# Two mixture layers behind a linear attention: the stretch around the second routing, reordered

## The chip, the core and the metric

One core of one Trainium2 chip runs the whole program. The metric is device microseconds of one execution; three runs of the kernel before are shown. The engines are PE (TensorE: matrix products, and transposes as products with an identity), DVE (VectorE), ACT (ScalarE), POOL (GpSimd) and SP (SyncE, which here issues DMAs). Each takes its own instructions in order, and waits on semaphores that the others and the DMAs raise.

## The reference, cut to what matters

The input goes through three layers. The first is a linear attention (8 x 8 heads, 576 positions, 64 wide) with a norm of each row. The second is a mixture of 8 experts in which each of 4608 tokens takes the expert with the highest score. The third is a mixture with a capacity:

```python
    cap = N // E
    logits = x @ w_gate
    order = np.argsort(-logits.flatten())
    ...
        if assigned[tok] >= 0 or counts[e] >= cap:
            continue
        assigned[tok] = e
    ...
        h = np.maximum(x[mask] @ w1[e], 0.0)
        out[mask] = h @ w2[e]
```

The third layer's assignment needs the logits of all tokens, so it needs the result of the second layer for all of them. "The second routing" is this assignment.

## The kernel before, in words

**Products.** Every fp32 product is made of three: hi x hi, lo x hi and hi x lo, of operands that are split into a rounded half (`whi`, `xh`, `hh`) and a rest (`wlo`, `xl`, `hl`). ACT makes the first halves, DVE the rests. A layer of an expert is `layer1_g` (lines 669 to 671, then relu) and `layer2_g` (lines 711 to 713, then a copy out of PSUM at line 717). An expert of the second layer has 608 slots, worked on in two chunks: chunk 0 has 256 columns (2 tiles of 128 rows), chunk 1 has 352 (3 tiles, the last of 96 rows). After a chunk's second layer, `rows_y` transposes the result back to rows (line 729), scales it (line 731), adds the token's number (line 732) and writes each tile to the buffer `ybuf` in HBM (line 734). The third layer gathers its rows from `ybuf` by a table of slots, `tab2`.

**The second routing.** It runs on DVE, with small products on PE between: `da_start` finds each expert's range of logits and spreads it to all partitions with a product (line 1060, operand `dg`); eight calls of `da_round` narrow a threshold per expert (2 of them, WARM, while the last expert's logits are not in yet, and 6, ROUNDS); `da_choice` takes the choice; `table2` makes the table, with three products for running counts (lines 1131 to 1133) and two halves of 20 products each (line 1167). The last instruction that makes the table is line 1182.

**What PE does meanwhile.** The second layers of the last two experts (e6 and e7, numbers 6 and 7) are kept back for this, in the generator `second()`; the last expert's first layers are in `first7()`. `stream` hands them out in pieces: a call `pe(us)` records products for about that many microseconds into PE's order, at that place. The tables TFILL, WFILL and PW say how much at which place. So the order of all engines is fixed when the program is built, by these numbers; the kernel uses no scheduler (`manual_schedule`). The splits of the last expert's hidden values (`hl`, line 1473) are DVE work that is put into the list LATER, and POPS says how many are taken out in each round, between the round's comparisons and its counts.

**The branch.** If the first assignment fails, a slow general way follows, in an `If` (line 1556) that is not entered with these inputs. All five engines load the flag, compare and branch past the body. `expect("gen")` marks a branch hint, which the program carries as an instruction at its start on the engines listed.

**After the branch.** POOL gathers the first expert's rows (five indirect DMAs, line 618), DVE makes three weight rests that were held back (line 550, list CAST), which frees the buffers for SP's next weight loads (line 528), PE runs `warm(NWARM)`: that many transposes of the identity (line 843) whose result nobody reads. Then the gathered tiles are transposed (line 636) and the third layer's first products follow.

Of the kernel before, what the change touches and what calls it, by code (L numbers as in the profile page):

```python
# [27 lines left out]

TFILL = (5.5, 0.35, 0.35, 2.0, 6.4, 100.0)

POPS = (1, 1, 2, 2, 2, 2)

WFILL = (4.2, 0.35, 0.35)

PW = (0, 0.8, 2.9, 2.1)

NWARM = 45

ASIDE = (1, 5, 5, 5, 3)

# [35 lines left out]
def fused_kernel(ctx, tc, q, k, v, g_norm, emb, tau, w1, w2, wgate, v1, v2, out):  # L76
# [28 lines left out]
    def mk(pool, shape, dtype, name, **kw):  # L105
        if pool is mp:
            pool = MP[name in MP0]
        return pool.tile(shape, dtype, name=name, **kw)
# [423 lines left out]
    def wcast(n=1, eng=None, ahead=3, later=None):  # L532
        for _ in range(n):
            if WS["cast"] >= len(WQ):
                return
            wload(WS["cast"] + 1)
            key = WQ[WS["cast"]][0]
            raw = RAW.pop(key)

            i = WS["cast"] // (RING // 2)  # L540
            wp = WP[(i + (i > 2 * E - 2)) % 2]
            hi = mk(wp, [128, 1024], F32R, "whi")
            lo = mk(wp, [128, 1024], F32R, "wlo")
            nc.scalar.copy(hi, raw)  # L544
            WT[key] = (hi, lo)
            WS["cast"] += 1
            up = WS["cast"] + ahead

            def rest(eng, lo=lo, raw=raw, hi=hi, up=up):
                eng.tensor_tensor(lo, raw, hi.bitcast(F32), op=OP.subtract)  # L550
                wload(up)
            if later is None:
                rest(eng or V)
            else:
                later.append(rest)
# [143 lines left out]
    def layer2_g(e, c, dp, mid=None):  # L699

        N = WID[0][c]
        if dp == 0:
            YT[e, c] = mk(mp, [128, KD, COLS[c]], F32, f"yT{c}")
        hh, hl = HT[0, e, c]
        ps = mk(psum, [128, 2, 512], F32, "mm")
        for t in range(2):
            o = ps[:, t, :N]
            d = (2 * dp + t) * 128
            for kf in range(KF):
                a, b = (w[:, d:d + 128] for w in wb(0, e, kf))  # L710
                nc.tensor.matmul(o, a, hh[:, kf, :N], start=(kf == 0), stop=False)  # L711
                nc.tensor.matmul(o, a, hl[:, kf, :N], start=False, stop=False)  # L712
                nc.tensor.matmul(o, b, hh[:, kf, :N], start=False, stop=(kf == KF - 1))  # L713
                yield 3 * N / 2400
            if mid and t == 0:
                mid()
        nc.scalar.copy(YT[e, c][:, 2 * dp:2 * dp + 2, :N], ps[:, :, :N])
# [4 lines left out]
    def rows_y(e, c, eng=V):  # L722

        y = YT[e, c]
        for (t, n) in tiles_of(c):
            o = 128 * t - 256 * c
            pt = mk(psum, [128, KD, 128], F32, "tp")
            for kd in range(KD):
                nc.tensor.transpose(pt[:n, kd, :], y[:, kd, o:o + n], ident)
            yr = mk(mp, [128, YP], F32, "yr", bufs=4)  # L730
            nc.scalar.activation(yr[:n, :HD], pt[:n].rearrange("p a b -> p (a b)"), AF.Copy, scale=gts[:n, e * SC + t:e * SC + t + 1])
            eng.tensor_copy(yr[:n, HD:].bitcast(I32), tabi[:n, e * SC + t:e * SC + t + 1].to_broadcast([n, YP - HD]))
            r0 = e * SL + 128 * t
            nc.sync.dma_start(ybuf[r0:r0 + n, :], yr[:n])
            yield 0.43
# [69 lines left out]
    def logits_w(e, c):  # L805
        N = WID[0][c]
        i = e - (E - ND)
        parts = [H7[0][:, :, 256 * c:256 * c + N]] if e == E - 1 else [h.bitcast(F32)[:, :, :N] for h in HT[0, e, c]]
        pl = mk(psum, [128, 512], F32, "sm")
        for kf in range(KF):  # L810
            g = kf % 4
            for x, p in enumerate(parts):
                nc.tensor.matmul(pl[32 * g:32 * g + 32, :N], W2G[0][:, i, kf - g:kf - g + 4, :].rearrange("p k e -> p (k e)"),
                                 p[:, kf, :], start=(kf < 4 and x == 0), stop=(kf >= 4 and x == len(parts) - 1),
                                 tile_position=(0, 32 * g))
        lgT = mk(mp, [128, C1 - 256], F32, "lgT")
        nc.scalar.copy(lgT[:, :N], pl[:, :N])
        return lambda: rows_l(e, c, lgT, 40)
# [5 lines left out]
    def stream(g):  # L824

        owed = [0.0]

        def pe(us):
            owed[0] += us
            while owed[0] > 0:  # L830
                d = next(g, None)
                if d is None:
                    owed[0] = 0.0
                    return
                owed[0] -= d
        return pe
# [113 lines left out]
    pe = stream(f0)  # L950
# [86 lines left out]
    def da_start(n, pe):  # L1037

        lm = mk(mp, [128, NCOL, E], F32, "rA")
        V.scalar_tensor_tensor(lm[:, :n], vneg[:, :n, None].to_broadcast([128, n, E]), -2.0, L[:, :n], op0=OP.mult, op1=OP.add)  # L1040
        mm = mk(mp, [128, 2, E], F32, "mmx")
        V.tensor_reduce(mm[:, 0], lm[:, :n].rearrange("p c e -> p e c"), axis=AX.X, op=OP.min)
        V.tensor_reduce(mm[:, 1], L[:, :n].rearrange("p c e -> p e c"), axis=AX.X, op=OP.max)
        pe(PW[3])
        pm = mk(psum, [128, 512], F32, "sm")
        for i in range(2):
            nc.tensor.transpose(pm[:E, 128 * i:128 * i + 128], mm[:, i], ident)
        V.tensor_reduce(st[:, 0:1], pm[:E, 0:128], axis=AX.X, op=OP.min)
        V.tensor_reduce(st[:, 3:4], pm[:E, 128:256], axis=AX.X, op=OP.max)
        V.tensor_tensor(st[:, 4:5], st[:, 3:4], st[:, 0:1], op=OP.subtract)  # L1050
        V.scalar_tensor_tensor(st[:, 0:1], st[:, 4:5], -0.25, st[:, 0:1], op0=OP.mult, op1=OP.add)
        V.tensor_scalar(st[:, 4:5], st[:, 4:5], 1.25, 1e-12, op0=OP.mult, op1=OP.max)
        V.reciprocal(st[:, 1:2], st[:, 4:5])
        V.tensor_scalar(st[:, 2:3], st[:, 4:5], 1.0 / J, None, op0=OP.mult)
        dg = mk(mp, [E, 3, E], F32, "dg")
        V.tensor_tensor(dg, ident[:E, None, :E].to_broadcast([E, 3, E]), st[:, 0:3, None].to_broadcast([E, 3, E]), op=OP.mult)
        ones8 = mk(mp, [128, NCOL, E], F32, "rB").rearrange("p a e -> p (a e)")[:E, :128]
        V.memset(ones8, 1.0)
        pb = mk(psum, [128, 512], F32, "sm")
        nc.tensor.matmul(pb[:, :3 * E], ones8, dg.rearrange("p a b -> p (a b)"), start=True, stop=True)  # L1060
        V.tensor_copy(lw.rearrange("p a b -> p (a b)"), pb[:, :3 * E])
# [324 lines left out]
    e6, e7 = E - 2, E - 1  # L1386
# [27 lines left out]
    def under(pe, t, asides, n=1):  # L1414
        def fill(i):
            for _ in range(0 if i else min(n, len(asides))):
                asides.pop(0)(V)
            pe(t[i])
        return fill
# [32 lines left out]
    pe = stream(f7)  # L1452
    pe(PW[2])
    da_start((E - 1) * SC, pe)
# [3 lines left out]

    def second():
        prev = None  # L1460
        for e, c in ((e6, 1), (e6, 0), (e7, 1), (e7, 0)):
            yield from layer2_g(e, c, 0)
            if prev is not None:
                yield from rows_y(*prev)
            yield from layer2_g(e, c, 1)
            prev = (e, c)
            if e == e6:
                N = WID[0][c]
                HT[0, e7, c] = [mk(mp, [128, KF, COLS[c]], F32R, f"h{p}{c}") for p in "hl"]
                for f in range(4):  # L1470
                    h, hh, hl = (x[:, 2 * f:2 * f + 2, o:o + N] for x, o in zip([H7[0], *HT[0, e7, c]], (256 * c, 0, 0)))
                    nc.scalar.copy(hh, h)
                    LATER.append(lambda eng, h=h, hh=hh, hl=hl: eng.tensor_tensor(hl, h, hh.bitcast(F32), op=OP.subtract))  # L1473
            if (e, c) == (e6, 0):
                wcast(3, later=CAST)
                while len(LATER) > 4:
                    LATER.pop(0)(V)
            if (e, c) == (e7, 1):
                while LATER:
                    LATER.pop(0)(V)  # L1480
        yield from rows_y(*prev)

    def expect(label):

        tc.mark_branch_hint_location(label, 0, engines=[mybir.EngineType.PE, mybir.EngineType.SP])

    s2_ = second()
    pe = stream(s2_)
    pe(PW[0])
    a = logits_w(e7, 1)  # L1490
    pe(PW[1])
    a()
    for r in range(ROUNDS):
        da_round(under(pe, TFILL, LATER, POPS[r]))
    da_choice()
# [118 lines left out]
    while CAST:  # L1614
        CAST.pop(0)(V)
    warm(NWARM)
    xtiles(1, 0, 0, 2)
# [50 lines left out]
```

## Time and profile before

| | us |
|---|---|
| median of 3 runs | 1119.45 |
| the three runs | 1116.06, 1119.45, 1123.03 |
| the profiled execution | 1119.71 |
| its span, first to last instruction | 1117.6 |
| around the span | 2.1 |

PE is busy for 95% of the span, DVE for 55%, ACT for 41%, POOL for 25%. The mean granted clock of PE is 0.976 of full speed; it shows 1.0 in most of the span, and 0.5 in a few short stretches. The stretch that the change touches lies between 550 and 690 us: the second routing runs from 551 to 666, the branch follows, and the third layer's first product starts at 681.3.

### The profile page before, as it was taken

The page shows a single profiled execution, that of the slowest core. Times are in us where ns is not written, and L with a number is a line of the kernel's source. Part 1 is how long each engine was busy: PE and PEld are TensorE (multiplying, and loading weights), DVE is VectorE, ACT ScalarE, POOL GpSimd, SP SyncE. Part 2 cuts the span into 40 slices and gives each one's busy share as a digit, 9 for nine tenths or more (in the row PEclk, how much of TensorE's full clock was granted, in tenths as well). Part 3 has the DMA queues.
Part 4 walks back from the last instruction along what each step waited for, and adds up shares of the span by engine and source line. Part 5 has one row for each costly group of instructions (what it writes and reads, how often), then busy time and mean ns, then how long its engine had stood idle before and what let it go on. Part 6 is the DMA issues. An engine that isn't in the chain of part 4 may idle for free. (4 is left out here: it accounts for less than half of the span.)

```text
span 1117.6 us, 20567 instructions
## 1 busy us (share of the span) xinstructions
PE 1061.9 (95%) x8380; PEld 982.8 (88%) x8380; DVE 617.1 (55%) x1275; ACT 453.7 (41%) x803; POOL 278.2 (25%) x363
## 2 busy tenths in 40 slices
PE   6988699999999999999999878999999999999998
PEld 6887698899999999999889768998989898989896
DVE  4467956777778786857557544433334242515140
ACT  2567536544445353545432222333324242414231
POOL 2011446516061423415001004030303030312101
PEclk9998799999999999999999998999999999999999
DMA  9999654443424243434111116334334342425201
GB/s 288 373 355 296 214 174 156 141 139 111 152 96 165 85 154 118 131 114 132 63 39 48 37 48 200 123 114 132 124 113 130 107 158 79 161 85 171 76 25 42
DMA packets 94517, 152.86 MB, mean 137 GB/s; under 512 B 11080, under 2 KB 52040, under 8 KB 94416
## 3 DMA queue, kind: packets, MB, share of 16 engines
q1 hardware_dynamic: 85456, 122.18, 33.0%
q0 software_dynamic: 8960, 29.30, 7.9%
q8 instruction: 67, 1.10, 0.4%
q14 instruction: 34, 0.28, 0.1%
HBM read 121.63 MB, written 29.82 MB: 136 GB/s over the span
## 5 line engine op out<-in xcount | busy, mean ns | idle before, releaser
L669 PE MATMUL mm<-xh,whi 128*128 128x256 f32 (+2 forms) x1024 | 312.6, 305 | 4.1 <-DVE hl L687 2.6
L670 PE MATMUL mm<-xl,whi 128*128 128x256 f32 (+2 forms) x1024 | 308.9, 302 | 1.0 <-DVE ti L646 0.7
L671 PE MATMUL mm<-xh,wlo 128*128 128x256 f32 (+2 forms) x1024 | 308.6, 301 | 0.0
L669 PEld LDWEIGHTS mm<-xh,whi 128*128 128x128 f32 x1024 | 196.0, 191 | 7.2 <-DVE hl L687 3.5
L670 PEld LDWEIGHTS mm<-xl,whi 128*128 128x128 f32 x1024 | 196.1, 191 | 1.7 <-DVE ti L646 1.1
L671 PEld LDWEIGHTS mm<-xh,wlo 128*128 128x128 f32 x1024 | 196.0, 191 | 0.0
L550 DVE TENSOR_TENSOR wlo<-wraw,whi 128x1024 fp32r<-128x1024 f32 x128 | 158.3, 1238 | 43.9 <-ACT whi L544 37.6
L711 PE MATMUL mm<-hh,whi 128*128 128x352 f32 (+1 forms) x512 | 160.0, 313 | 1.0 <-DVE rA L1138 1.0
L712 PE MATMUL mm<-hl,whi 128*128 128x352 f32 (+1 forms) x512 | 156.1, 305 | 3.8 <-DVE hl L1473 3.5
L713 PE MATMUL mm<-hh,wlo 128*128 128x352 f32 (+1 forms) x512 | 156.0, 305 | 0.0
L640 DVE TENSOR_TENSOR xl<-tp,xh 128x512 fp32r<-128x512 f32 (+2 forms) x80 | 51.5, 649 | 187.5 <-ACT xh L639 187.5
L544 ACT CAST whi<-wraw 128x1024 fp32r<-128x1024 f32 x128 | 133.4, 1044 | 0.0
L1606 POOL DMA_INDIRECT out<-yr,ti x40 | 39.3, 983 | 313.4 <-ACT yr L1604 291.1
L801 DVE SCALAR_TENSOR_TENSOR rc<-xg,big 128x512 bf16<-128x512 f32 x128 | 111.1, 868 | 2.6
L686 ACT ACTIVATE hh<-mm 128x512 fp32r<-128x512 f32 (+1 forms) x88 | 57.2, 650 | 113.0 <-PE mm L671 113.0
L712 PEld LDWEIGHTS mm<-hl,whi 128*128 128x128 f32 x512 | 98.5, 192 | 4.4 <-DVE hl L1473 3.8
L1593 PE MATMUL mm<-whi,hh 128*128 128x512 f32 x256 | 101.0, 394 | 0.0
L711 PEld LDWEIGHTS mm<-hh,whi 128*128 128x128 f32 x512 | 98.2, 192 | 2.9 <-DVE rA L1138 1.3
L1595 PE MATMUL mm<-whi,hl 128*128 128x512 f32 x256 | 100.4, 392 | 0.0
L1594 PE MATMUL mm<-wlo,hh 128*128 128x512 f32 x256 | 100.3, 392 | 0.0
L713 PEld LDWEIGHTS mm<-hh,wlo 128*128 128x128 f32 x512 | 98.3, 192 | 0.0
L687 DVE SCALAR_TENSOR_TENSOR hl<-mm,hh 128x512 fp32r<-128x512 f32 (+1 forms) x88 | 66.0, 750 | 48.5 <-ACT hh L686 48.3
(282 smaller groups left out, 1461.2 us busy)
## 6 DMA issues: line engine op xcount, KB each, us to landing
wraw<-in_moe_w SPq DMA_DIRECT2D x128, 512.0 KB, 3.8
kmain<-in_k SPq DMA_DIRECT2D x16, 576.0 KB, 10.7
vmain<-in_v SPq DMA_DIRECT2D x16, 576.0 KB, 11.1
xbuf<-xo SPq DMA_DIRECT2D x16, 528.0 KB, 7.4
ybuf<-yr SPq DMA_DIRECT2D x32, 260.0 KB, 2.5
qmain<-in_q SPq DMA_DIRECT2D x16, 512.0 KB, 10.9
xg<-in_moe_w SPq DMA_DIRECT2D x16, 256.0 KB, 3.9
xg<-in_moe_w_gate SPq DMA_DIRECT2D x8, 256.0 KB, 3.8
```

The costliest lines, as they stand in the source:

```text
L544: nc.scalar.copy(hi, raw)
L550: eng.tensor_tensor(lo, raw, hi.bitcast(F32), op=OP.subtract)
L669: nc.tensor.matmul(o, a, xh[:, kd, :N], start=(kd == 0), stop=False)
L670: nc.tensor.matmul(o, a, xl[:, kd, :N], start=False, stop=False)
L671: nc.tensor.matmul(o, b, xh[:, kd, :N], start=False, stop=(kd == KD - 1))
L711: nc.tensor.matmul(o, a, hh[:, kf, :N], start=(kf == 0), stop=False)
L712: nc.tensor.matmul(o, a, hl[:, kf, :N], start=False, stop=False)
L713: nc.tensor.matmul(o, b, hh[:, kf, :N], start=False, stop=(kf == KF - 1))
L801: V.scalar_tensor_tensor(junk, raws[i], 1.0, wgB[:, x], op0=OP.mult, op1=OP.mult, accum_out=w2g[:, i // KF, i % KF, x:x + 1])
L1593: nc.tensor.matmul(ps[:n, i, :], hh, a, start=(kf == 0), stop=False)
L1594: nc.tensor.matmul(ps[:n, i, :], hh, b, start=False, stop=False)
L1595: nc.tensor.matmul(ps[:n, i, :], hl, a, start=False, stop=(kf == KF - 1))
```

## The change

It has five parts. (1) `da_start` records about 2.0 us of products (PW[4]) between the range and the broadcast product. (2) `second()` takes the kept-back chunks in the order 0, 1, 0, 1 instead of 1, 0, 1, 0; the two places that depend on it follow. (3) POPS has 1 instead of 2 for the fifth round. (4) The hint is marked on ACT, DVE and POOL too, not only on PE and SP. (5) NWARM is 28, not 45.

```diff
-POPS = (1, 1, 2, 2, 2, 2)
+POPS = (1, 1, 2, 2, 1, 2)
-PW = (0, 0.8, 2.9, 2.1)
+PW = (0, 0.8, 2.9, 2.1, 2.0)
-NWARM = 45
+NWARM = 28
@@ da_start
         V.tensor_scalar(st[:, 2:3], st[:, 4:5], 1.0 / J, None, op0=OP.mult)
+        pe(PW[4])
         dg = mk(mp, [E, 3, E], F32, "dg")
@@ second
-        for e, c in ((e6, 1), (e6, 0), (e7, 1), (e7, 0)):
+        for e, c in ((e6, 0), (e6, 1), (e7, 0), (e7, 1)):
...
-            if (e, c) == (e6, 0):
+            if (e, c) == (e6, 1):
                 wcast(3, later=CAST)
                 while len(LATER) > 4:
                     LATER.pop(0)(V)
-            if (e, c) == (e7, 1):
+            if (e, c) == (e7, 0):
                 while LATER:
                     LATER.pop(0)(V)
@@ expect
-        tc.mark_branch_hint_location(label, 0, engines=[mybir.EngineType.PE, mybir.EngineType.SP])
+        tc.mark_branch_hint_location(label, 0, engines=[mybir.EngineType[n] for n in ("PE", "SP", "Activation", "DVE", "Pool")])
```

From line 1055 on, a line of the changed kernel has a number that is one higher.

The first place is PE's order in `da_start`, at the broadcast product (a piece of the difference; the rows between its two parts are the same in both).

```order
 L671 MATMUL mm<-xh_6483,wlo 128x256
 L1047 MATMUL sm<-ident,mmx 8x128 x2
-L1060 MATMUL sm<-dg,rB 128x24
 L669 MATMUL mm<-xh_6483,whi 128x256
 L670 MATMUL mm<-xl_6484,whi 128x256
@@ -2948,4 +2947,5 @@
 L670 MATMUL mm<-xl_6484,whi 128x256
 L671 MATMUL mm<-xh_6483,wlo 128x256
+L1061 MATMUL sm<-dg,rB 128x24
 L669 MATMUL mm<-xh_6483,whi 128x256
```

The broadcast product moved behind 15 products of 256 columns and four transposes of 96 rows, all of which stood behind it before.

The second place is DVE's order in a round in which PE waits for the split hidden values. Before, in the fourth round (`hl_7251` is chunk 1 of the last expert):

```order
L1084 SCALAR_TENSOR_TENSOR rB<-rB,rP 128x320
L1087 TENSOR_REDUCE ru<-rB 128x40
L1090 TENSOR_TENSOR rc<-ru,gridf 128x32x20 x2
L1473 TENSOR_TENSOR hl_7251<-big,hh_7250 128x704 x2
L1098 COPY rB<-sm 32x128
L1103 TENSOR_SCALAR jk<-sm 32x8
```

With the change, in the sixth and last round (`hl_7434` is the same chunk):

```order
L1085 SCALAR_TENSOR_TENSOR rB<-rB,rP 128x320
L1088 TENSOR_REDUCE ru<-rB 128x40
L1091 TENSOR_TENSOR rc<-ru,gridf 128x32x20 x2
L1474 TENSOR_TENSOR hl_7434<-big,hh_7433 128x704 x3
L1099 COPY rB<-sm 32x128
L1104 TENSOR_SCALAR jk<-sm 32x8
```

Three of that chunk's four pieces are now made here; PE's first product with `hl_7434` stands shortly before this round's counts, where before its first product with `hl_7251` stood right behind the third round's.

The third place is SP's order ahead of the branch. Before:

```order
L528 DMA wraw<-in_moe_w 128x4x256 x3
L734 DMA ybuf<-yr 128x520 x2
L734 DMA ybuf<-yr 96x520
L734 DMA ybuf<-yr 128x520 x4
L734 DMA ybuf<-yr 96x520
L734 DMA ybuf<-yr 128x520 x2
L1556 TENSOR_LOAD fli
```

With the change:

```order
L528 DMA wraw<-in_moe_w 128x4x256 x3
L734 DMA ybuf<-yr 128x520 x4
L734 DMA ybuf<-yr 96x520
L734 DMA ybuf<-yr 128x520 x4
L734 DMA ybuf<-yr 96x520
L1557 TENSOR_LOAD fli
```

The last chunk written before the branch is now the one with three tiles, the last of 96 rows.

## Rows read from the trace of the kernel before

**Rows 1.** The page: the span, and PE's busy time.

```profile
span 1117.6 us, 20567 instructions
...
PE 1061.9 (95%) x8380; PEld 982.8 (88%) x8380; DVE 617.1 (55%) x1275; ACT 453.7 (41%) x803; POOL 278.2 (25%) x363
```

**Rows 2.** Timeline at the broadcast: start, duration, instruction, [idle before <- releaser].

```profile
554.87 0.17 DVE L1058 MEMSET rB<- 8x128 f32 x1
...
555.18 0.37 PE L1060 MATMUL sm<-dg,rB 8*128 8x24 f32 x2 [1.78 <-DVE rB L1058]
```

**Rows 3.** Timeline in the fourth round: the hidden values' rest, and PE.

```profile
624.11 1.69 DVE L1473 TENSOR_TENSOR hl<-big,hh 128x704 fp32r<-128x704 f32 x2
...
625.05 0.66 PE L712 MATMUL mm<-hl,whi 128*128 128x352 f32 x1 [3.46 <-DVE hl L1473]
```

**Rows 4.** Timeline of PE at the table's first products.

```profile
644.78 0.72 PE L1131 MATMUL mm<-Pf,ones 128*128 128x320 bf16 x1 [0.65 <-DVE Pf L1071]
...
647.94 0.39 PE L711 MATMUL mm<-hh,whi 128*128 128x256 f32 x1 [0.96 <-DVE rA L1138]
```

**Rows 5.** Windows: stretch; length, busy by engine, then PEclk, DMA share, GB/s.

```profile
556.00:561.00 5.00, 5.00 (x31) 4.99 (x30) 4.42 (x9) 1.72 (x5) 1.26 (x2) 0.66 0.01 2
624.00:629.00 5.00, 3.95 (x16) 3.95 (x17) 1.80 (x3) 0.71 (x1) 0.00 (x0) 0.66 0.00 0
648.00:653.00 5.00, 5.00 (x29) 5.00 (x30) 4.79 (x12) 1.59 (x2) 0.00 (x0) 0.66 0.00 0
...
682.00:687.00 5.00, 4.96 (x29) 4.96 (x30) 1.27 (x2) 0.61 (x2) 1.05 (x2) 0.66 0.28 107
...
670.00:675.00 5.00, 4.96 (x24) 4.99 (x25) 3.50 (x3) 0.00 (x0) 3.53 (x3) 0.50 0.53 157
676.00:677.80 1.80, 1.80 (x19) 1.80 (x18) 0.00 (x0) 0.00 (x0) 1.50 (x2) 1.00 0.98 327
```

**Rows 6.** Timeline around the last chunk ahead of the branch, on ACT, PE and SP.

```profile
658.00 0.68 ACT L731 ACTIVATE yr<-tp,gts 96x512 f32<-96x512 f32 x1
...
656.84 0.62 PE L729 MATMUL tp<-ident,yT 128*96 128x128 f32 x4
...
665.64 0.32 SPq L734 DMA_DIRECT2D ybuf<-yr  x1
```

**Rows 7.** Line 1556, the branch, by sequencer: durations ns min/median/max, first and last start.

```profile
L1556 SPq EVENT_SEMAPHORE  x9: 17/17/17, 667.5 to 669.9; - x9
...
L1556 PEldq EVENT_SEMAPHORE  x2: 51/51/51, 665.7 to 665.8; - x2
...
L1556 DVEq EVENT_SEMAPHORE  x2: 21/21/21, 669.9 to 670.0; - x2
...
L1556 PEldq COMPARE_BRANCH  x1: 397/397/397, 665.2 to 665.2; - x1
...
L1556 DVEq COMPARE_BRANCH  x1: 72/72/72, 666.7 to 666.7; - x1
...
L1556 SPq COMPARE_BRANCH  x1: 70/70/70, 667.0 to 667.0; - x1
```

**Rows 8.** Waits of SP's queue, 655 to 690: us in total, times, longest.

```profile
SPq L1556 <- SPq L1556: 2.3, 2, 1.9
```

**Rows 9.** Timelines of DVE, PE, POOL and SP from the table's end on.

```profile
665.79 0.20 DVE L1182 SCALAR_TENSOR_TENSOR tab<-si 128x40 int32<-128x40 f32 x1
...
670.04 7.98 PE L843 MATMUL sm<-ident 128*128 128x128 f32 x45 [4.62 <-DVEq L1556]
...
679.99 0.66 PE L636 MATMUL tp<-ident,xg 128*128 128x128 f32 x4 [1.53 <-DMA xg<-ybuf,tab]
681.32 0.39 PE L669 MATMUL mm<-xh,whi 128*128 128x256 f32 x1 [0.68 <-ACT xh L639]
...
670.86 1.34 POOL L618 DMA_INDIRECT xg<-ybuf,tab  x1 [34.87 <-SPq L1556]
...
671.34 0.40 SPq L528 DMA_DIRECT2D wraw<-in_moe_w  x1
```

**Rows 10.** The chain that ended last, at the gather: start, us, what.

```profile
672.51 7.43 DMA xg<-ybuf,tab
```

## The prediction

> **What bounds the kernel now.** I read the page first: PE is busy for 1061.9 of the span's 1117.6 us [rows 1], so the kernel can only get shorter by what PE loses, which is idle time and time at the lower of its two clock levels (granted 0.5, 1.2 GHz, against 1.0, 2.4 GHz). Then I went through the timeline of PE between 551 and 690 us for its idle times, and through the windows of the same stretch for the granted clock. There are three holes: 1.78 us before the broadcast product [rows 2], 3.46 us before the first product with the split hidden values [rows 3], and 0.65 and 0.96 us at the table's first products [rows 4]. After each hole the clock falls: the five microseconds around each show a granted clock of 0.66, with PE busy for all of them or for all but the hole [rows 5]. A window of 5 us at 0.66 does 3.3 us of work at full clock, so 1.7 us are lost beside the hole itself. The fourth place is the branch: PE has nothing for 4.62 us and later waits 1.53 us for the gathered rows [rows 9]. The times are of one execution, of 1119.7 us; the median of the three runs is 1119.45, so the sum against the one is good for the other.
>
> The kept-back products are a fixed amount of work, and the last fill takes what is left of them. So a product that is put into an early hole shortens the end by its own time, as long as DVE's chain does not become the later one. PE's holes up to the table are 6.9 us in 115, so DVE keeps pace with PE, but not by much; that is the rivals' business.
>
> **(a) Products ahead of the broadcast: gain 3.5.** DVE's last preparation ends at 555.04, PE's product starts at 555.18, after a hole of 1.78 [rows 2]. The 2.0 us of products that now stand ahead fill it, and the broadcast runs about 0.2 us later, which DVE waits. The hole goes (1.8), and with it the low clock behind it (1.7) [rows 5]. The bounds are 1.8 (the clock falls anyway) and 3.5; I take the upper one, because in the rows the fall comes behind a hole.
>
> **(b) Second layers in the order 0, 1, 0, 1: gain 5.0.** Before, DVE makes two pieces of `hl` in 1.69 us, 0.85 each, and PE's product starts only when the first is ready [rows 3], because chunk 1 of the last expert is needed in the round in which it is split. With the change chunk 0 of the last expert comes first, whose pieces are taken out earlier, and chunk 1 is split up to the last round. The hole goes (3.46), and the low clock behind it: 1.7, of which about 0.15 lies in the hole's last 0.3 us (half a clock for 0.3 us) and must not be counted twice, so 1.55. The bounds are 0 (a hole of the same size opens in the last round) and 5.0. DVE's work is moved, not added: the fifth round takes one piece fewer, the sixth makes three, 2.5 us.
>
> **(c) The table: gain 2.65.** The hole of 0.65 is a fill that is too short for DVE's `Pf`; that fill is unchanged, and it stays. The hole of 0.96 lies at a chunk's first product, which waited for a `rA` buffer's reader at line 1138 [rows 4]; with the new order no chunk starts there. It goes, and I let the clock behind it (0.66 from 648 to 653 [rows 5]) go too: 0.96 + 1.7. The bounds are 0 and 2.65, since the 0.65 that stays stands 3 us ahead of that stretch and might pull the clock down alone.
>
> **(d) The last chunk is the longer one: loss 0.5.** Ahead of the branch PE, ACT and SP now end with the tile of 96 rows as a third one. Its transposes take 0.62 on PE and its scaling 0.68 on ACT [rows 6]; they follow each other, but ACT's overlaps the next work of PE, and one more `ybuf` write goes out on SP. Between 0 and 1.3; I take 0.5.
>
> **(e) Hints on ACT, DVE and POOL: gain 1.5.** DVE, not hinted, compares at 666.7 and goes on at 669.9, 3.2 us; SP, hinted, goes from 667.0 to 667.5, and PE from 665.2 to 665.7, 0.5 us each [rows 7]. So a hint is worth up to 2.7 us on the engine that gets it. POOL's gather starts at 670.86, 4.87 us after the table's end at 665.99, and PE's transposes start at 670.04, released by DVE [rows 9]. But DVE is not alone: SP too waited at the branch, 1.9 us at the longest, and its last step there is also at 669.9 [rows 7, 8], 4.3 us after it issued the last `ybuf` write [rows 6]; the gather reads `ybuf`, so it can't go before that has landed. If that wait follows the landing, nothing is gained; if it follows the other engines, or a transfer that their late instruction loads held up, 2.7. Between 0 and 2.7 I take 1.5, a little over the middle, because SP's last step and DVE's first fall into the same tenth of a microsecond.
>
> The Trainium skill speaks against this part: "Runtime: NRT & Kernel Launch", section "Instruction fetch mechanics", says that prefetch is purely sequential and that a taken branch to outside of the window forces a fetch before execution goes on. By that rule no mark could help, and the time would be that of the second case below. The trace differs: the two hinted engines go on after 0.5 us, the unhinted one after 3.2.
>
> **(f) Weight loads against the gather: nothing, within 1.** The second gather takes 7.43 us to land [rows 10]; SP's next weight load is issued at 671.34, after the first gather's start at 670.86 [rows 9], 1.4 us behind DVE's restart. DVE's rests free those buffers, so an earlier DVE brings the loads forward, and the gathers must share: the DMA engines are busy for 0.53 and then 0.98 of the time [rows 5]. I let POOL and DVE move together, so that the order stays.
>
> **(g) 28 transposes for 45: loss 0.85.** The 45 take 7.98 us; PE then waits 1.53 for the gathered rows, not for the transposes, before the gathered tiles at 679.99 [rows 9]. So leaving out 17 shortens nothing: the gather covers them all. It lengthens the idle time before the third layer by 1.6 us at full clock (17 at 1.80 / 19, the stretch from 676.0 [rows 5]), or up to 3.0 at the mean of both clocks (17 at 7.98 / 45). The products after it ran at 0.66 already [rows 5], a loss of 1.7; if the clock now stays low twice as long, 1.7 more. Between 0 and 1.7, 0.85.
>
> Another size comes from the Trainium skill: "TensorE: Matmul & The Clock Gate", section "Part 4: PE-mode transpose", holds that transposes don't count as PE work for the clock. By it this part costs 0. The trace disagrees: PE ran only the filling transposes from 670 on, at 0.50 first and at 1.00 between 676.0 and 677.8 [rows 5].
>
> **Sum.** Other short falls of the clock may come elsewhere in the reordered rounds: 0.5 off. 3.5 + 5.0 + 2.65 - 0.5 + 1.5 - 0.85 - 0.5 = 10.8, and 1119.7 - 10.8 = 1108.9, which I round to 1109.0. A measurement of this kernel can tell about 1%, 11.2 us, from no change; the line to "faster" is 1108.3, almost at my forecast.
>
> **Rivals.**
> - *Forecast*, chance 0.58, own range 1104.5 to 1113.
> - *The hints move nothing*: the landing of the last `ybuf` write ends last, whatever DVE does. For it: SP's wait of 1.9 us [rows 8]. Against: DVE's restart releases PE directly [rows 9]. (e) is 0: 1110.4. Chance 0.2.
> - *Weight loads pass the gathers*: DVE restarts early and POOL, which must wait for `ybuf`, does not; the 512 KB loads fill the queues first. At 327 GB/s [rows 5] three loads are 1.57 MB or 4.8 us, of which part is hidden: second gather 4 us later, 1108.9 + 4 = 1112.9. Chance 0.12.
> - *Slower: the last chunk's rests come late.* Three of the four pieces of chunk 1 are made in the sixth round, behind its comparisons. If PE comes to its first product with them before DVE has, it stands, and the round's counts, queued behind on PE, stand too; DVE waits for those, and the table after it. One such hole costs what the old one did, 3.46 + 1.55 = 5.0 [rows 3, 5], and takes back (b): 1113.9. Slower than before it is from a third such hole on (10.8 / 5.0 is 2.2), one for each late piece: 1108.9 + 15 = 1123.9. For it: DVE has three pieces in one place, 2.5 us. Against: PE has all of chunk 0's second layer ahead of them. Chance 0.05, mostly of one hole.
> - *Transposes don't count for the clock*: (g) is 0, 1108.0. For it nothing in the rows but that products follow at 0.66; the 1.00 [rows 5] is against it. Chance 0.05.
>
> The range is 1103.5 to 1114.5: upward it takes in the second and third case and one hole; downward the whole 2.7 of (e), no loss in (d), (f) and (g), and 1 us less to load behind the gather. Chances: faster about half of the forecast and of the last case, and a fifth of the second, with a share for gains that I took short, 0.40; slower 0.04, from late pieces and from what I have not seen; within 1% the rest, 0.56.
>
> **What would show it.** (a): no hole over 0.7 before the broadcast product, granted clock 1.0 behind it. (b): no wait of line 712 (now 713) on `hl`. (c): one hole at the table, of 0.65. (e): DVE goes on 0.5 us after its branch, and the time from the table's end to POOL's gather falls from 4.87 towards 2.2; if it stays, the second case holds. (f): the second gather lands in more than 7.4 us, with loads issued ahead of it. (g): idle time of PE between the 28 transposes and the gathered tiles, and a granted clock under 0.66 in the first 5 us of products. Wrong I would be above all if DVE's chain is the later one once the holes are filled: then they come back in other rounds, of other names.

## The result, and the profile after

The changed kernel takes 1108.76 us (median of 7 runs, 1104.60 to 1112.90); the kernel before, timed beside it, 1120.64 (7 runs, 1116.06 to 1123.03). The ratio is 0.9896, with a 95% interval of 0.9869 to 0.9923: some 1% faster, 11.9 us between the medians. Timed again, unedited (`after_again`, below), it was 0.9905 [0.9884, 0.9925]. The profiled execution is the one of 1108.76; its span is 1106.8, 10.8 shorter than that of before [rows 1].

The page's span and the busy times:

```profile
span 1106.8 us, 20535 instructions
...
PE 1052.8 (95%) x8363; PEld 973.2 (88%) x8363; DVE 617.3 (56%) x1275; ACT 453.4 (41%) x803; POOL 276.6 (25%) x363
```

Timelines of the three places of [rows 2 to 4] in the changed kernel (start, duration, instruction, idle before and releaser):

```profile
557.21 0.17 DVE L1059 MEMSET rB<- 8x128 f32 x1
...
557.52 0.37 PE L1061 MATMUL sm<-dg,rB 8*128 8x24 f32 x2 [0.18 <-DVE rB L1059]
...
638.13 0.72 PE L1132 MATMUL mm<-Pf,ones 128*128 128x320 bf16 x1 [0.19 <-DVE Pf L1072]
```

The hole of 1.78 before the broadcast is 0.18. Line 713's wait on `hl` is gone: no idle time of PE between 565 and 650 is over 0.4. At the table the hole of 0.65, which I had let stand, shrank to 0.19, and the one of 0.96 is gone. Windows of the same places, in the columns of [rows 5]; the last is the third layer's start:

```profile
558.00:563.00 5.00, 5.00 (x36) 4.78 (x36) 4.64 (x12) 0.78 (x3) 0.88 (x1) 1.00 0.01 2
620.00:625.00 5.00, 5.00 (x48) 4.71 (x47) 3.79 (x9) 3.71 (x6) 0.64 (x1) 1.00 0.00 2
641.00:646.00 5.00, 5.00 (x35) 4.98 (x35) 4.76 (x10) 1.71 (x3) 0.00 (x0) 1.00 0.00 0
...
670.40:675.40 5.00, 4.81 (x23) 4.53 (x24) 1.98 (x3) 0.93 (x1) 1.55 (x2) 0.57 0.26 96
```

The granted clock is 1.00 where it was 0.66; only at the third layer's start is it low, 0.57, as it was before (0.66). Then the branch and what follows, timelines of DVE, PE and POOL, which answer to [rows 9]:

```profile
656.95 0.20 DVE L1183 SCALAR_TENSOR_TENSOR tab<-si 128x40 int32<-128x40 f32 x1
...
659.61 2.05 POOL L618 DMA_INDIRECT xg<-ybuf,tab  x1 [30.54 <-SPq L1557]
...
658.35 3.25 PE L843 MATMUL sm<-ident 128*128 128x128 f32 x28 [1.78 <-DVEq L1557]
666.89 1.12 PE L636 MATMUL tp<-ident,xg 128*128 128x128 f32 x4 [5.29 <-DMA xg<-ybuf,tab]
668.65 1.11 PE L636 MATMUL tp<-ident,xg 128*128 128x128 f32 x4 [0.64 <-DMA xg<-ybuf,tab]
670.44 0.58 PE L669 MATMUL mm<-xh,whi 128*128 128x256 f32 x1 [0.67 <-ACT xh L639]
```

And the branch itself by sequencer ([rows 7]), SP's longest wait there ([rows 8]) and the chain that ended last ([rows 10]):

```profile
L1557 SPq EVENT_SEMAPHORE  x9: 17/17/17, 658.4 to 659.0; - x9
...
L1557 DVEq EVENT_SEMAPHORE  x2: 21/21/21, 658.2 to 658.3; - x2
...
L1557 DVEq COMPARE_BRANCH  x1: 84/84/84, 657.6 to 657.6; - x1
...
SPq L1557 <- SPq L1557: 0.5, 1, 0.5
...
656.65 2.16 DMA ybuf<-yr
...
661.96 6.64 DMA xg<-ybuf,tab
```

DVE goes on 0.6 us after its compare (3.2 before), and SP's wait of 1.9 is 0.5. The gather starts 2.46 after the table's end instead of 4.87. The chain now runs through the landing of the last `ybuf` write, 2.16 us after its issue; before, SP's wait ended 4.3 us after it.

Cut at the same five points, the two traces give the budget. "Routing" starts with DVE's reduction at line 1043 (before, then after):

```profile
552.43 0.64 DVE L1043 TENSOR_REDUCE mmx<-L 128x8 f32<-128x280 f32 x1
```

```profile
554.23 0.64 DVE L1043 TENSOR_REDUCE mmx<-L 128x8 f32<-128x280 f32 x1
```

| stretch | before | after | difference |
|---|---|---|---|
| start of program to routing | 552.43 | 554.23 | +1.80 |
| routing to table's end | 113.56 | 102.92 | -10.64 |
| table's end to first gather | 4.87 | 2.46 | -2.41 |
| first gather to third layer's first product | 10.46 | 10.83 | +0.37 |
| that product to the end | 436.28 | 436.36 | +0.08 |
| span | 1117.60 | 1106.80 | -10.80 |

The first row is not put down to the change: in the profiles of this study the routing starts anywhere from 549.6 to 555.0. So single terms are read from the stretches below, not from whole times: the median of the kernel before alone went from 1118.32 to 1120.64 between four measurements.

### The profile page after: what moved, and what is told of

The parts are those of the page before. It is cut to its first block, busy times and chain, and to the rows that moved or that the text cites. A ratio compares the mean times of both kernels' runs of the same rounds, so it can differ in the third digit from the quotient of the medians.

```text
span 1106.8 us, 20535 instructions
## 1 busy us (share of the span) xinstructions
PE 1052.8 (95%) x8363; PEld 973.2 (88%) x8363; DVE 617.3 (56%) x1275; ACT 453.4 (41%) x803; POOL 276.6 (25%) x363
## 4 chain that ended last, share of the span: by engine, by line
PE 54%; issue 20%; POOL 4%; DVE 2%; DMA 1%; POOLq 1%; ACT 1%; ACTq 0%
PE mm L669 8%; PE mm L670 8%; PE mm L671 8%; PE mm L711 6%; PE mm L713 6%; PE mm L712 6%; PE mm L1596 2%; PE mm L1594 2%; PE mm L1595 2%; PE tp L636 2%; POOL out L1607 2%; POOL xg L618 2%; PE tp L729 1%; PE mm L1588 1%; PE sm L813 1%
```

## The experiments

All ratios are to the kernel before, on the same chip. "Table" is the stretch from the routing's start to the table's end, "gather" that from there to POOL's first gather.

| run | time, us | ratio [95%] | table | gather |
|---|---|---|---|---|
| before (profile) | 1120.64 | | 113.56 | 4.87 |
| changed (profile) | 1108.76 | 0.9896 [0.9869, 0.9923] | 102.92 | 2.46 |
| a_nopw | 1113.75 | 0.9943 [0.9920, 0.9966] | 106.26 | 2.55 |
| a_oldorder | 1116.78 | 0.9972 [0.9953, 0.9991] | 109.11 | 4.76 |
| a_oldhint | 1110.68 | 0.9917 [0.9893, 0.9941] | 102.87 | 4.60 |
| a_warm45 | 1108.30 | 0.9905 [0.9878, 0.9933] | 102.97 | 2.50 |
| b_hint | 1119.26 | 1.0011 [0.9997, 1.0025] | 112.24 | 4.71 |
| b_order | 1113.11 | 0.9956 [0.9939, 0.9973] | 106.07 | 4.62 |
| t_delay | 1117.95 | 0.9999 [0.9981, 1.0016] | 111.54 | 4.79 |
| t_delay2 | 1116.45 | 0.9982 [0.9962, 1.0001] | 110.38 | 3.68 |
| v_late | 1106.21 | 0.9888 [0.9869, 0.9908] | 102.84 | 2.62 |
| v_late0 | 1106.17 | 0.9891 [0.9866, 0.9915] | 102.92 | 2.58 |
| after_again | 1108.52 | 0.9905 [0.9884, 0.9925] | 102.79 | 2.62 |
| a_warm0 | 1108.50 | 0.9912 [0.9886, 0.9938] | 102.98 | 2.58 |

### One part undone

**a_nopw.** No products ahead of the broadcast.

```diff
-PW = (0, 0.8, 2.9, 2.1, 2.0)
+PW = (0, 0.8, 2.9, 2.1, 0)
```

> The changed kernel without the 2.0 us of products ahead of the broadcast product (PW[4] = 0), the rest as changed. Theory 1 (a hole costs itself and the low clock behind it, and the fixed rest of the kept-back products hands it on to the end): a hole of about 1.8 us before the broadcast product, a granted clock near 0.66 in the 5 us behind it, and 3.5 us more from the start of the routing (line 1043's reduction) to the table's end, which was 102.9 us (554.23 to 657.15) in the changed kernel: 106.4. Whole time about 1112. Theory 2 (DVE's rounds set the pace, PE's hole is made up for in a later wait): the hole is there, but the table ends less than 1 us later, and the whole time stays at 1109. Theory 3 (the hole counts, the clock doesn't fall behind it): 1.3 to 1.8 more, 1110.5.

The table ends 3.34 later (106.26 against 102.92), as theory 1 says, but not by its mechanism. PE's timeline, then the window behind the hole:

```profile
557.00 0.37 PE L1061 MATMUL sm<-dg,rB 8*128 8x24 f32 x2 [1.78 <-DVE rB L1059]
562.56 0.43 PE L670 MATMUL mm<-xl,whi 128*128 128x352 f32 x1 [1.28 <-DVE xl L640]
...
556.00:561.00 5.00, 4.00 (x34) 4.00 (x34) 4.07 (x13) 1.58 (x4) 1.26 (x2) 1.00 0.00 0
```

The hole of 1.78 is back, the clock stays at 1.00, and instead PE runs into a second hole, 1.28 us for DVE's rest `xl`. In the profile of before the clock fell here [rows 5], and PE, slower, had no such hole. `b_hint` and `b_order` have the same hole of 1.78, a clock of 1.00 and a second hole of 1.25 and 1.27. So one price has two shapes: PE at the low clock, or PE at the full clock waiting for DVE. The two holes make up 2.9 of the 3.34 us here (1.78 less the 0.18 that stayed, and 1.28); what the rest is has not been shown.

**a_oldorder.** The second layers in the order 1, 0, 1, 0.

```diff
-        for e, c in ((e6, 0), (e6, 1), (e7, 0), (e7, 1)):
+        for e, c in ((e6, 1), (e6, 0), (e7, 1), (e7, 0)):
...
-POPS = (1, 1, 2, 2, 1, 2)
+POPS = (1, 1, 2, 2, 2, 2)
```

> The changed kernel with the second layers in the old order 1, 0, 1, 0, and the old POPS; the other three parts as changed. Theory 1: the 3.46 us hole at the split hidden values and the 0.96 us hole at the table are back, with a granted clock near 0.66 behind each; less the shorter last chunk this is 5.0 + 2.65 - 0.5 = 7.1 us more from the start of the routing to the table's end (102.9 becomes 110), whole time about 1116. Theory 2 (the two holes are an accident of the old alignment; with the 2.0 us of products ahead of the broadcast PE comes later to them): holes of under 2 us in all, 2 to 3 us more, 1111.5.

The table ends 6.2 later (theory 1: 7.1). PE's timeline, the windows behind the two holes, and then the branch and POOL:

```profile
621.08 0.43 PE L712 MATMUL mm<-hl,whi 128*128 128x352 f32 x1 [3.47 <-DVE hl L1474]
...
644.14 0.38 PE L711 MATMUL mm<-hh,whi 128*128 128x256 f32 x1 [0.96 <-DVE rA L1139]
...
621.00:626.00 5.00, 4.92 (x21) 4.92 (x22) 0.83 (x2) 0.00 (x0) 0.00 (x0) 0.66 0.00 0
644.00:649.00 5.00, 4.86 (x40) 4.86 (x41) 4.76 (x10) 1.60 (x2) 0.00 (x0) 1.00 0.00 0
...
L1557 SPq EVENT_SEMAPHORE  x9: 17/17/17, 662.3 to 664.7; - x9
...
L1557 DVEq EVENT_SEMAPHORE  x2: 21/21/21, 662.0 to 662.2; - x2
...
665.50 1.15 POOL L618 DMA_INDIRECT xg<-ybuf,tab  x1 [33.31 <-SPq L1557]
```

Both holes return, but the clock falls behind the longer one alone. What none of my theories had is the end: DVE is hinted and goes on at 662.0, yet the gather starts 4.76 us after the table's end, as in the kernel before, because SP is held until 664.7. With the old order the hints give next to nothing (4.76 against 4.87). No run undoes the order without POPS, or brings back one of the two holes without the other, so these stand as one part.

**a_oldhint.** The hint on PE and SP alone.

```diff
-        ... engines=[mybir.EngineType[n] for n in ("PE", "SP", "Activation", "DVE", "Pool")])
+        ... engines=[mybir.EngineType.PE, mybir.EngineType.SP])
```

> The changed kernel with the hint on PE and SP alone. Theory 1 (the late restart of DVE holds up the gather): DVE goes on 3.2 us after its branch instead of 0.6, the gather starts 4.9 us after the table's end instead of 2.46, whole time 2.4 us more, 1111.2. Theory 2 (the last write of the buffer ybuf sets the gather, and it lands 2.2 us after its issue whatever the hints say): DVE's restart is late, but the gather still starts 2.5 us after the table's end, and the time is 1109. Theory 3 (the instruction loads of the unhinted engines lie on the same DMA engines as the write and hold it up): SP's wait at the branch is long again (1.9 us), the gather late by 2.4.

```profile
L1557 SPq EVENT_SEMAPHORE  x9: 17/17/17, 656.6 to 657.4; - x9
...
L1557 DVEq EVENT_SEMAPHORE  x2: 21/21/21, 659.0 to 659.1; - x2
...
659.98 1.35 POOL L618 DMA_INDIRECT xg<-ybuf,tab  x1 [32.55 <-DVEq L1557]
```

Theory 1: the gather starts 4.60 after the table's end, and its releaser is now DVE, which goes on at 659.0; SP had been done at 657.4, so theories 2 and 3 fall. The time is 1.9 us more, 1110.68; the intervals of the two ratios overlap, so it is the trace that shows the loss.

**a_warm45** and **a_warm0.** 45 filling transposes, and none.

```diff
-NWARM = 28
+NWARM = 45
```

> The changed kernel with 45 filling transposes instead of 28. Theory 1 (the gather covers them, the shorter idle time behind them lets the clock rise sooner): the gathered tiles' transposes start at the same time after the gather's start (7.3 us), PE's idle time before them falls from 5.29 to 2 or 3 us, and the granted clock in the first 5 us of the third layer's products is above the 0.63 of the changed kernel; 0.5 to 1.5 us less time, 1107.5 to 1108.5. Theory 2 (the number of filling transposes has no effect, since they don't count for the clock): 1108.8, the clock as with 28. Theory 3 (45 are too many once the gather is early): PE's transposes end after the gathered rows are there, up to 1 us more, 1110.

> The changed kernel without any filling transposes after the branch. 45 instead of 28 had no effect. Theory 1 (PE's clock is low at the third layer's start with 28 anyway, since 5 us of idle time follow them): without any, the clock at the gathered tiles is the same 0.50, the first 5 us of products the same 0.5 to 0.6, the time 1108.8. Theory 2 (even 28 shorten the low stretch): the clock rises some us later than with 28, up to 1.5 us more, 1110.

Windows of the third layer's first 5 us, with 45 and then, of the other kernel, with none:

```profile
667.90:672.90 5.00, 4.85 (x23) 4.56 (x24) 1.93 (x3) 0.87 (x1) 1.91 (x2) 0.55 0.30 107
```

```profile
668.90:673.90 5.00, 4.85 (x24) 4.56 (x25) 1.94 (x3) 0.88 (x1) 1.90 (x2) 0.59 0.35 100
```

The clock there is 0.55 with 45, 0.57 with 28 (above) and 0.59 with none; the times are 1108.3, 1108.8 and 1108.5. The number of filling transposes has no effect here that these times can show, and the clock moves no more than between two executions of the unedited kernel (0.57, and 0.52 in `after_again`). With 45, PE's wait ahead of the gathered tiles does fall, from 5.29 to 2.10, as theory 1 said, but PE still waits for the rows, and the clock is low behind that wait all the same.

### One part alone: two waits, both of which must go

**b_hint** is the kernel before with the five hints; **b_order** is the kernel before with the new order and POPS (the edits above, the other way round).

> The kernel before with the hint marked on ACT, DVE and POOL too, nothing else. Theory 1 (the gather waits for two things, DVE's restart and the landing of the last ybuf write; in the old order of chunks the write ends last, 4.2 us after its issue, since PE's and the others' instruction loads come 1.1 to 1.3 us after the issue and share its DMA engines): DVE goes on 0.6 us after its branch, but the gather still starts 4.8 us after the table's end, and the time is that of before, 1119.5. Theory 2 (the hint is worth what taking it away cost, 2 us, whatever the order): gather 2.5 to 3 us after the table's end, 1117.5. On the holes: if the fall of the clock belongs to them, the 5 us behind each of the three holes show about 0.66 again; in other runs the clock stayed at 1.00 behind a hole of 1.78 and one of 0.96 and fell behind the one of 3.46, so I expect 0.66 surely behind that one alone.

> The kernel before with the new order of the second layers and the new POPS, nothing else. Theory 1 (two waits): from the routing's start to the table's end 106.3 us instead of 113.6; the last ybuf write, of 96 rows, lands about 2.2 us after its issue, but DVE restarts 3.1 us after its branch, so that the gather starts 4.6 us after the table's end: the order gives 7 us by the routing alone, 1112.5. Theory 2 (the early landing is enough): gather 2.5 us after the table's end, 1110.5. Theory 3 (the order's gain comes only with the products ahead of the broadcast, which set PE against DVE's rounds): table's end over 110 us, new holes at the split hidden values, 1116 or more.

POOL's first gather, in b_hint and then in b_order:

```profile
670.23 1.19 POOL L618 DMA_INDIRECT xg<-ybuf,tab  x1 [33.24 <-SPq L1556]
```

```profile
663.77 1.35 POOL L618 DMA_INDIRECT xg<-ybuf,tab  x1 [32.58 <-DVEq L1556]
```

Theory 1 holds both times. The hints alone gain nothing (1.0011 [0.9997, 1.0025]): the gather starts 4.71 us after the table's end, released by SP. The order alone gives the table's 7 us, but the gather starts after 4.62, released by DVE. Together it is 2.46. The gather starts behind the later of two waits, and each part removes one of them. In b_hint the clock behind the holes of 1.78 and 0.96 was 1.00, behind the one of 3.47 it was 0.66, as expected.

### Why the last write lands late in the old order

The trace has a record of each DMA packet: its queue, start, duration and size. No view lists them one by one. They show the last rows of the last `ybuf` write, and beside them instruction loads, on queues of that name: packets of 16,384 bytes, 1.0 to 1.9 us each, and of 8,192 bytes, 0.3 to 1.3 us. A load of 16,384 bytes starts 1.6 to 1.9 us behind PE's compare in each profile looked at, wherever that lies, so it is taken for PE's. In b_hint the first loads start at 666.27 and 666.54, while the rows of the last two writes are under way (from 665.41 on); the last row ends at 668.89. In the changed kernel the write has 96 rows in its last tile, the loads start at 658.28, and the last row ends at 658.41.

**t_delay** and **t_delay2** test whether the loads are the cause: the old order, with work added ahead of the branch so that PE's and ACT's loads come later.

```diff
+    junk = con([128, 32], F32, "junk")
     table2(under(pe, TFILL[3:], LATER, 2), general)
+    warm(12)     # t_delay2: warm(30)
+    for _ in range(7):
+        nc.scalar.copy(junk, ident[:, :32])
```

> The kernel with the old order of the second layers (its table's end at 109.1 us, its gather 4.76 us behind that, 1116.8 us), and ahead of the branch 12 more filling transposes on PE and 7 small copies on ACT, which nobody reads. Theory 1 (the instruction loads of PE and ACT, 1.1 to 1.3 us after the last ybuf write's issue, hold that write up): both engines branch 1.2 us later, their instruction loads come after the write has landed, it lands about 2.3 us after its issue, and the gather starts 2.5 to 3 us after the table's end: some 2 us less, 1114.8, though work was added. Theory 2 (a write of 128 rows takes 4.2 us here whatever else runs): the gather stays at 4.8 us after the table's end, the time at 1116.8 or up to 1.2 more.

> The kernel with the old order and added work ahead of the branch, with 30 filling transposes on PE instead of 12 (the 7 small copies on ACT stay). With 12, all packets of the last ybuf write but one had landed 2.0 us after its issue, and that one came at 3.3 us, right behind PE's 16 KB instruction load that started 1.9 us after the issue. Theory 1 (the instruction loads hold the write up): with 30, PE's load comes 2 us later, the write lands whole at 2.0 to 2.3 us, and the gather starts 2.5 to 3.3 us after the table's end instead of 4.8; PE's filling work doesn't delay it. Time some 1.5 us less than with the old order alone, 1115.3. Theory 2 (something else ends the wait, a fixed time of about 4.8 us in the old order): gather at 4.8 us again, 1117.

With 12, the 16 KB load starts at 662.93; all rows but one have landed by then or 0.01 later, and that one's record starts at 663.97, where the load's ends, and ends at 664.34. The gather is no sooner, so the expectation missed: the delay was too short for one row. With 30, no instruction load starts before 661.88, the last row ends at 661.40, 1.8 us after the write's issue, and SP is done at 662.1. The landing is settled: in the same order the write takes 1.8 us without instruction loads beside it (659.64 to 661.40), 3.8 with them (660.39 to 664.17 in a_oldorder). But the gather starts only 3.68 after the table's end. Rows of t_delay2, the branch and POOL:

```profile
L1561 SPq EVENT_SEMAPHORE  x9: 17/17/17, 661.5 to 662.1; - x9
...
L1561 PEldq EVENT_SEMAPHORE  x2: 51/51/51, 662.8 to 663.0; - x2
...
663.67 1.09 POOL L618 DMA_INDIRECT xg<-ybuf,tab  x1 [33.68 <-PEq L1561]
```

The releaser is PE, which the added work had made late. So the expectation that PE's work would not delay the gather was wrong: in these profiles the gather follows the last engine through the branch, whichever it is, and the write. Adding work moved it 1.1 us sooner; the times (1116.45 against 1116.78) don't tell the two apart.

### The weight loads beside the gather

**v_late** puts two of the three held-back weight rests behind the gathered tiles' rests on DVE, so that their 512 KB loads go out later; **v_late0** all three.

```diff
     gather(1, 0)
-    while CAST:
-        CAST.pop(0)(V)
+    CAST.pop(0)(V)          # v_late0: without this line
     warm(NWARM)
     xtiles(1, 0, 0, 2)
+    while CAST:
+        CAST.pop(0)(V)
     wcast()
```

> The changed kernel with the second and third of the three weight rests that were held back (line 550) put behind the first two gathered tiles' rests on DVE instead of ahead of them; so only one 512 KB weight load is issued beside the gather, not three. Theory 1 (the weight loads share the DMA engines with the gather and make it late): the second gather lands 2 to 3 us sooner (4 to 4.5 us after its issue instead of 6.6), the third layer's first product starts as much sooner, and the time is 1106.5, if the weights that are loaded later are not missed. Theory 2 (the gather's 6.6 us are its own): it lands as before, 1108.8. Theory 3 (the later weight loads are missed): the gather sooner, but waits of PE or ACT for weights before 700 us, 1108.8 or more.

> The changed kernel with all three held-back weight rests (line 550) behind the first two gathered tiles' rests on DVE, so that no weight load runs beside the gather; with two of them behind, the second gather landed 4.8 us after its issue instead of 6.6, and the kernel took 1106.2 us. Theory 1 (each load beside the gather costs): another 0.5 to 1.5 us sooner for the gather; but the first rest is now needed by the third product of the third layer and takes 1.23 us of DVE behind the gathered tiles, so PE waits about 1 us there: 1105.5 to 1106.7. Theory 2 (one load doesn't matter): gather as with two behind, PE waits 1 us for the rest, 1107.2.

DVE's first rest, the first two gathers and the first product in v_late, and then the second gather and the product that waits in v_late0:

```profile
659.15 1.23 DVE L550 TENSOR_TENSOR wlo<-wraw,whi 128x1024 fp32r<-128x1024 f32 x1 [1.27 <-DVEq L1557]
...
660.50 1.02 POOL L618 DMA_INDIRECT xg<-ybuf,tab  x1 [30.57 <-DVE wlo L550]
...
661.82 4.80 DMA xg<-ybuf,tab
...
668.00 0.39 PE L669 MATMUL mm<-xh,whi 128*128 128x256 f32 x1 [0.68 <-ACT xh L639]
```

```profile
658.52 4.83 DMA xg<-ybuf,tab
...
667.11 0.58 PE L671 MATMUL mm<-xh,wlo 128*128 128x256 f32 x1 [0.61 <-DVE wlo L550]
```

With one load beside it instead of three the second gather lands 4.80 us after its issue instead of 6.64, and the time from the first gather to the first product is 7.5 instead of 10.8. That is theory 1 for v_late, but the loads are not all of the 3.3 us. The landing is 1.84 of it. Another 1.03 is the start of the second gather, 1.32 us behind the first instead of 2.35: POOL's instruction for the first took 1.02 instead of 2.05. In the changed kernel DVE's three rests run beside it:

```profile
658.40 3.50 DVE L550 TENSOR_TENSOR wlo<-wraw,whi 128x1024 fp32r<-128x1024 f32 x3 [1.26 <-DVEq L1557]
```

Of the 560 such instructions of the third layer in the 14 profiles, the 352 that started with no rest under way took 0.90 to 1.02 us, and the others 0.78 to 0.91 us plus what was left of the rest: 1.09 with 0.20 left (t_delay2), 1.35 with 0.45 (a_oldhint), 1.90 with 1.00 (after_again), 2.05 with 1.16 (the changed kernel). The weight loads don't do this: the later gathers, with the loads still running, took 0.95. The last 0.46 us is PE's, whose transposes of the second tile took 0.66 in v_late and 1.11 in the changed kernel.

Without any load the second gather lands after 4.83: theory 2 for v_late0, the first load costs it nothing, and PE waits 0.61 for the rest it now lacks. The time, 1106.17, lies where theory 1 had put it, but the intervals are too wide to decide by it.

**after_again** is the changed kernel itself, on the same chip as v_late0:

> The changed kernel itself, unedited, to compare the others of this call with, and to see what of its profile comes again. All theories: 1108.8; from the routing's start to the table's end 102.9 us, granted clock 1.00 in it throughout, gather 2.5 us after the table's end, second gather 6.6 us after its issue.

Table (102.79), gather (2.62) and clock (1.00 throughout the routing) came as expected; the second gather took 6.93 us, not 6.6. With three loads beside it, it took 6.64 to 7.26 in the changed kernel and the runs that leave its hints and its order as they are. v_late and v_late0 have the lowest medians here, 2.3 us under this one; the intervals of the ratios overlap, so the times alone don't show them faster than the changed kernel, while the trace shows v_late's first product 3.2 us sooner after the table. Both beat the kernel before.

## Why the prediction was right, point by point

The forecast was 1109.0, the result 1108.76, in the range, and the case that I had held likeliest, (a) to (g) as written, gave it. But its terms were right unevenly.

- **(a)**, 3.5: the runs with and without it differ by 3.34 (a_nopw) and 3.20 (b_order against a_oldhint). It was right in size; the half that I put on the clock is the clock in some executions and a second hole in others.
- **(b) + (c) - (d)**, 7.15: between 6.2 and 8.6 by the tables of a_oldorder, t_delay2 and t_delay against the changed kernel's. The long hole and its low clock were there in each of the five profiles with the old order. The spread is (c): behind the hole of 0.96 the window's clock was 1.00, 0.67 and 0.51 in those three, though the instructions up to the table are the same. I had taken its 1.7 whole, the upper one of my bounds. How the sum divides between (b) and (c) no run shows. What I let stand at the table, 0.65, became 0.19.
- **(d)**, a loss of 0.5: about right in the tail, where PE's idle time grew by 0.55 (0.62 + 0.39 against 0.46). What I had not seen is that the same shift gains at the branch: the last write, of 96 rows, is issued 1.63 us ahead of the first instruction load (1.1 in a_oldorder) and has landed but for 0.13 us when that starts; this lets (e) pay.
- **(e)**, a gain of 1.5: 2.41 in the profiles, 2.1 by a_oldhint, none by itself (b_hint). My two bounds were two waits that must both go; I took a mean between them where it was one or the other, decided by the order of chunks. The rival "the hints move nothing", 0.2, is what holds for the hints alone, and by the mechanism given there; with the new order it fell. The Trainium skill, "Runtime: NRT & Kernel Launch", section "Instruction fetch mechanics", has each sequencer fetch instructions by DMA in blocks of 16 KiB and calls the cost of crossing a block boundary mostly hidden. The trace agrees on the block in the packets of 16,384 bytes, which moved with PE's branch in t_delay2; others were of 8,192. What such loads cost here behind the branch was 2 us of a data write beside them (3.8 against 1.8).
- **(f)**, nothing within 1: the second gather took 6.64 after 7.43. That is no gain either: before, it was the second gather's own instruction that met a rest of DVE (1.89 us), now it is the first's (2.05), and from the first gather to the landing of the second it is 9.08 before and 8.99 after. The mechanism of the rival is real (v_late: 1.84 us), but it was there before the change too.
- **(g)**, a loss of 0.85: none, nor for 0 or 45 transposes. Both signs that I had named came, idle time of 5.29 behind the transposes and a clock of 0.57, but with 45 and an idle time of 2.10 the clock was 0.55, so it does not come from the number. The rival by which transposes don't count for the clock had the same size (0). Its reason isn't needed, for PE waits for rows behind the transposes in all three, and one row speaks against it: in a_warm45 PE ran nothing but these transposes from 655.53 to 662.19, and the granted clock was 0.50 from 655.6 to 658.6 and 1.00 from 658.8 to 662.0. The 0.5 for other falls of the clock did not come either.

By the stretches the change gave 12.6 in the two profiles (10.64 + 2.41 - 0.37 - 0.08), against 10.8: 0.5 more in the routing, 0.9 more at the branch, 0.4 less lost behind it. The medians give 11.0 to 11.9. That the spans differ by just 10.8 is partly luck, the 1.8 us that the changed execution lost ahead of the routing. The rival of the other sign, late rests in the last round, did not come: PE's longest wait between the sixth round's parts was 0.24.

## What to carry to other kernels

Where two waits end within a few tenths of a microsecond of each other, price a change of either one at nothing until the other goes too, and look for the second in the same change; a mean between "nothing" and "all" hits neither. What a short low clock behind a hole costs belongs partly to the single execution: take it surely behind the long hole only, and see whether PE at full speed would just meet the next late operand. At a branch that all engines pass, look at what the DMA engines carry beside the instruction loads, and issue the last write that matters early enough to be done. Where POOL issues gathers, see what DVE runs at that moment: the order of a few rests of 1.2 us decided here when the second gather went out.

## What the hardware showed that I had not expected

- Instruction loads can hold up data: a `ybuf` write lasted 3.8 us from issue to its last row with a 16 KB load (1.05 us) and an 8 KB load (1.30 us) under way, 1.8 without; in t_delay one row alone was late, and started where the 16 KB load ended (663.97).
- The same hole of 0.96 in the same order of instructions was followed by a granted clock of 1.00 in two profiles (a_oldorder, b_hint), of 0.51 to 0.67 in three (before, t_delay, t_delay2).
- One 512 KB load beside the gathers cost the second one nothing (4.80 against 4.83); three cost 1.84 (6.64), up to 2.5 in other profiles (7.26).
- POOL's instruction for an indirect gather stood while a DVE weight rest was under way: 2.05 us with 1.16 of the rest left, 1.09 with 0.20, 1.02 with none.
